# Q and K by DMA transpose, all inputs in 384-byte rows, and K^T V a unit ahead, in a gated linear attention + maxout kernel

## Chip, cores and metric

One core of one Trainium2 chip. The time is the device time of one execution in microseconds (us); lower is better. A run whose time is over 1.5% above the fastest of the same kernel is called slow, and ratios use the fast runs alone.

## The reference

Per batch and head, a 48 x 48 state is decayed by alpha and fed by the outer product of k and v at each of 768 steps; y is q times the state. The result, as 3072 tokens of 384 values, goes through a maxout layer.

```python
def _attn_ref(q, k, v, alpha):                     # (4, 8, 768, 48) each
    for t in range(S):
        state = alpha[:, :, t, :, None] * state + einsum('bhd,bhe->bhde', k[:, :, t], v[:, :, t])
        y[:, :, t] = einsum('bhd,bhde->bhe', q[:, :, t], state)
def _moe_ref(x, w1, w2, w_out):                    # (3072, 384), d_ff 1024
    return np.maximum(x @ w1, x @ w2) @ w_out
```

## The kernel before

The work is cut into 12 units of 256 tokens (two chunks of 128). A unit's chain: Ln of alpha on ScalarE; cumulative sums by matmul with masks; Exps; K and Q scaled (GpSimd, VectorE); **transposes of K and Q on TensorE**; pairs K Q^T ("pp", TensorE), masked on VectorE; K^T V for the state; y ("ya"); y transposed ("xp"); and, for the unit before, the hidden layer ("hp", 4 groups, each emptied by a Relu) and the output ("op"). The program order on each engine is fixed by hand, and all loads are issued by SyncE, four units ahead.

From unit 2 on, K and Q are loaded in 192-byte rows, so that each lands with one chunk on 128 partitions; alpha, V and the first units come in 384-byte rows (two tokens a row).

```python
def load_rows(u, name, src, cc):                   # 192-B rows: K, Q of units >= 2
    ...
    for j in range(2):
        nc.sync.dma_start(out=t[name][64 * j : 64 * j + 64, cc],
            in_=rows(src, u, cc * C, C).rearrange("h (p j) d -> j p h d", j=2)[j])

def turn(u, cc):                                   # 8 TensorE transposes and a PSUM copy
    tp = new(f"g{cc if u else 2 + cc}", [128, 2, HP, C], FP16, 1, "tp")
    for n, src in ((1, X["kn"][cc]), (0, X["qn"][cc])):
        for j in range(HP):
            nc.tensor.transpose(tp[:, n, j, :], pair(src, j), ident)
    ...

for u in range(2, NU):                             # one turn
    if u + 4 < NU:
        load(u + 4)
    kvmm(u, 0); pmm(u, 0); ...                     # K^T V, pairs of unit u
    hid(u - 1, 0); hid(u - 1, 1)                   # hidden layer of unit u-1
    sumd(u + 1); hid(u - 1, 2); sumc(u + 1); ...   # sums and Exps of unit u+1
    pmm(u, 1); ystate(u); ...
    hid(u - 1, 3, True)
    ...                                            # K, Q of u+1 scaled
    outp(u - 1, 0); yin(u)
    turn(u + 1, 0); turn(u + 1, 1)                 # transposes of unit u+1
    ...
```

## Time and profile before

| | before |
|---|---|
| time, median (range) | 146.35 us (145.24 to 147.23), 3 runs |
| span of the profiled run | 143.6 us |
| mean granted TensorE clock | 1.00 |
| TensorE busy | 94% |
| DMA queue of SyncE, share of 16 engines | 85.9% |

I call a **turn** the time from the first matmul of one unit's sums ("cs<-halves") to that of the next. In before, the turns of the loop (u = 2 to 9) take 9.66, 9.66, 9.77, 9.76, 9.76, 9.60, 9.59, 9.59 us.

### The profile page before, as it was taken

Reading aid. Unit: us, or ns where it says so; the run is one execution under the profiler, and the core shown is the slowest. Engines: PE = TensorE matmul, PEld = TensorE weight load, DVE = VectorE, ACT = ScalarE, POOL = GpSimd, SP = SyncE. Lnnn points to the kernel's source line nnn. Section 1 sums busy time; section 2 is a strip of 40 time slices with the busy share of each in tenths; the row PEclk is TensorE's granted clock in tenths of the full one; section 3 lists DMA queues with packets and bytes.
Section 4 is the critical chain, followed back from the end, with each engine's and each line's share of the span. In section 5 each row is a group of like instructions: output and inputs, shape, how many; then the busy total and the mean of one; then the engine's idle time right before and its main releaser. Section 6 shows DMA issues by size and latency. Waiting matters only on the chain.

```text
span 143.6 us, 4259 instructions
## 1 busy us (share of the span) xinstructions
PE 134.4 (94%) x1689; PEld 97.1 (68%) x1689; DVE 87.4 (61%) x180; ACT 97.1 (68%) x200; POOL 56.6 (39%) x111
## 2 busy tenths in 40 slices
PE   6868879998999999999999999999999999999991
PEld 2335544764877767877877777778777777776770
DVE  6048892865976757766767677556675755571110
ACT  3467642398788688687786975896879767655520
POOL 7491442066436154182291461631913616310000
PEclk9999999999999999999999999999999999999999
DMA  3999999978999999997998989999999785020203
GB/s 98 271 360 321 296 370 347 264 126 184 226 152 254 167 277 178 194 187 136 253 206 172 290 141 206 269 172 294 155 214 242 134 246 226 0 110 5 110 0 110
DMA packets 76483, 28.58 MB, mean 199 GB/s; under 512 B 71728, under 2 KB 74672, under 8 KB 76464
## 3 DMA queue, kind: packets, MB, share of 16 engines
q1 hardware_dynamic: 76320, 28.22, 85.9%
q8 instruction: 13, 0.21, 0.6%
q10 hardware_dynamic: 144, 0.10, 0.2%
q14 instruction: 6, 0.05, 0.1%
HBM read 23.59 MB, written 4.72 MB: 197 GB/s over the span
## 4 chain that ended last, share of the span: by engine, by line
PE 76%; SPq 10%; DMA 6%; ACT 3%; DVE 1%; issue 1%; ACTq 0%
PE hp L410 23%; PE op L435 20%; PE op L429 8%; SPq L75 6%; PE tp L296 6%; DMA w1f<-in_moe_w_dram 6%; PE pp L345 4%; PE ya L381 3%; PE cs L237 3%; PE xp L397 3%; PE kv L318 2%; SPq L115 2%; SPq L121 1%; PE ya L369 1%; PE cs L223 1%; ACT gT L415 1%
## 5 line engine op out<-in xcount | busy, mean ns | idle before, releaser
L415 ACT ACTIVATE gT<-hp 128x512 f16<-128x512 f32 x47 | 28.1, 597 | 16.2 <-PE hp L410 15.5
L410 PE MATMUL hp<-xt,w 128*128 128x256 f16 x288 | 37.4, 273 | 0.4 <-DVE w L498 0.2
L351 DVE TENSOR_TENSOR pt<-pp,um 128x512 f16<-128x512 f32 x48 | 30.9, 686 | 9.7 <-PE pp L345 9.4
L435 PE MATMUL op<-wo,gT 128*128 128x384 f16 x184 | 34.0, 326 | 0.0
L285 POOL TENSOR_TENSOR kn<-kf,Em 128x384 f16<-128x384 f32 x24 | 23.4, 996 | 24.8 <-ACT Em L247 24.8
L410 PEld LDWEIGHTS <-w 128*128 128x128 f16 x288 | 25.9, 97 | 5.3 <-issue 0.9
L435 PEld LDWEIGHTS <-gT 128*128 128x128 f16 x184 | 17.5, 98 | 10.5
L277 POOL TENSOR_TENSOR sb<-tm,dd 128x192 f16<-128x192 f32 x20 | 10.1, 506 | 32.5 <-DVE tm L331 20.2
L439 ACT COPY outs<-op 128x384 f32<-128x384 f32 x23 | 11.0, 477 | 13.7 <-PE op L435 13.7
L289 DVE TENSOR_TENSOR qn<-qf,cs 128x384 f16<-128x384 f32 x24 | 12.3, 550 | 13.0 <-ACT de L257 12.1
L331 DVE TENSOR_TENSOR tm<-kv,sb 64x192 f32<-64x192 f32 x32 | 11.3, 353 | 8.8 <-PE kv L318 7.9
L303 DVE COPY qk<-tp 128x1024 f16<-128x1024 f16 x20 | 12.9, 686 | 4.3 <-PE tp L296 4.3
L429 PE MATMUL op<-w2o,xt 128*128 128x384 f16 x69 | 15.0, 326 | 0.0
L205 POOL CAST v<-vf 64x384 f16<-64x384 f32 x24 | 12.0, 501 | 7.5 <-DMA vf<-in_v_dram 6.6
L207 ACT CAST v<-vf 64x384 f16<-64x384 f32 x24 | 12.2, 510 | 1.9 <-DMA vf<-in_v_dram 1.4
L247 ACT ACTIVATE Em<-cs 128x384 f32<-128x384 f32 x24 | 11.6, 485 | 2.5 <-PE cs L237 2.5
L193 ACT ACTIVATE lg<-af 128x768 f16<-128x768 f32 x12 | 10.1, 843 | 3.3 <-DMA af<-in_alpha_dram 3.0
L252 ACT ACTIVATE cs<-cs 128x384 f32<-128x384 f32 x24 | 11.8, 494 | 0.0
L504 PE MATMUL warm<-wz 128*128 128x512 f16 x30 | 10.0, 447 | 1.3 <-DVE halves L149 1.3
L388 ACT CAST xn<-ya 128x384 f16<-128x384 f32 x24 | 10.4, 492 | 0.0
L296 PE MATMUL tp<-ident,kn 128*128 128x128 f16 x96 | 9.3, 218 | 1.0 <-DVE qn L289 0.5
L345 PE MATMUL pp<-qk 48*128 48x128 f16 x192 | 9.8, 217 | 0.4 <-DVE qk L301 0.4
(66 smaller groups left out, 155.3 us busy)
## 6 DMA issues: line engine op xcount, KB each, us to landing
af<-in_alpha_dram SPq DMA_DIRECT2D x12, 384.0 KB, 5.6
vf<-in_v_dram SPq DMA_DIRECT2D x12, 384.0 KB, 5.0
out_dram<-outs SPq DMA_DIRECT2D x11, 384.0 KB, 5.1
kf<-in_k_dram SPq DMA_DIRECT2D x40, 96.0 KB, 4.7
qf<-in_q_dram SPq DMA_DIRECT2D x40, 96.0 KB, 4.3
w2f<-in_moe_w_dram SPq DMA_DIRECT2D x3, 512.0 KB, 6.0
wof<-in_moe_w_out_dram SPq DMA_DIRECT2D x2, 768.0 KB, 8.3
w1f<-in_moe_w_dram SPq DMA_DIRECT2D x4, 384.0 KB, 9.7
```

Source lines behind the costliest of these rows:

```text
L205: nc.gpsimd.tensor_copy(out=o, in_=i)
L207: nc.scalar.copy(out=o, in_=i)
L285: nc.gpsimd.tensor_mul(out=X["kn"][cc][:, :, 0:D], in0=part(u, "kf", cc), in1=X["Em"][cc])
L289: nc.vector.tensor_mul(out=X["qn"][cc][:, :, 0:D], in0=part(u, "qf", cc), in1=X["csv"][cc])
L296: nc.tensor.transpose(tp[:, n, j, :], pair(src, j), ident)
L303: nc.vector.tensor_copy(out=X["qk"][:, cc], in_=tp.rearrange("p n h t -> p (n h) t"))
L345: nc.tensor.matmul(pa[a][:, j, :], lhsT=qk[r, 1, j, :], rhs=qk[r, 0, j, :], start=True, stop=True)
L351: nc.vector.tensor_mul(out=pt[:, a], in0=X["pa", cc][a], in1=um.unsqueeze(1).to_broadcast([128, HP, C]))
L410: nc.tensor.matmul(hp[:, n, :], lhsT=w12[:, ds, f * 128 : (f + 1) * 128], rhs=X["xt"][:, ds].rearrange("p n t -> p (n t)"), start=(ds == 0 ...
L415: nc.scalar.activation(out=gT[:, 2 * f2 : 2 * f2 + 2, :], in_=hp, func=ACTF.Relu)
L429: nc.tensor.matmul(op, lhsT=X["xt"][:, ds, n, :], rhs=w2o[:, ds, :], start=(ds == 0), stop=False)
L435: nc.tensor.matmul(op, lhsT=X["gT"][:, f, n * C : (n + 1) * C], rhs=wo16[:, f, :], start=False, stop=(f == NF - 1))
```

## The change

Intent: take 16 transposes a unit (0.90 us) from TensorE, which bounds the kernel, by letting the DMA transpose K and Q from unit 3 on; load K and Q in the 384-byte rows that move faster; and compute K^T V a unit ahead, so that the state is there when y wants it. For the DMA transposes to land in time, sums and Exps of the next unit move to the head of a turn. Core of the diff (the loop cut to its order):

```diff
-    PAIRED = (0, 1)
+    BY_PE = (0, 1, 2)
...
-    def load_kq(u, cc):
-        load_rows(u, "kf", k, cc)
-        load_rows(u, "qf", q, cc)
+    def load_kq(u):
+        load_fat(u, "kf", k)
+        load_fat(u, "qf", q)
...
+                m = mf[:, j, i].rearrange("p c t -> p (c t)")
+                nc.tensor.matmul(csv[i], lhsT=m, rhs=lg[:, j, :, 0:D], start=(j == 0), stop=(j == 1))
...
+        if u in BY_PE:
+            ...
         else:
-            nc.vector.tensor_copy(out=X["qk"][:, cc], in_=tp.rearrange("p n h t -> p (n h) t"))
+            for cc in range(2):
+                nc.sync.dma_start(
+                    out=X["qk"][:, cc, :, 64 * i : 64 * i + 64],
+                    in_=X["kq"][64 * cc : 64 * cc + 64, i].rearrange("p n h w -> p (n h w)"), transpose=True,
+                )
...
     for u in range(2, NU):
         if u + 4 < NU:
-            load(u + 4)
+            load_a(u + 4)
+            load_kq(u + 4)
         if nxt:
-            sumd(u + 1)
+            sums(u + 1)
             expm(u + 1, 0)
             expp(u + 1, 0)
             expm(u + 1, 1)
+        pmm(u, 0)
...
+        hid(u - 1, 0, True)
+            kmul(u + 1, 0); qmul(u + 1, 0); expp(u + 1, 1); turn(u + 1, 0)
+        hid(u - 1, 1, True)
+            kmul(u + 1, 1); qmul(u + 1, 1); turn(u + 1, 1); expd(u + 1)
...
+        hid(u - 1, 2, True)
+        pmm(u, 1)
+            kvmm(u + 1)
+        if u + 4 < NU:
+            load_v(u + 4)
         hid(u - 1, 3, True)
...
-                ln(u + 2)
+        if u + 3 < NU:
+            ln(u + 3)
```

(Before the loop, `ln(3)` and `ln(4)`. The lines with semicolons stand for several of the diff. The rows of two tokens also ask for a third copy of V in every unit, on GpSimd, in unit 3 on VectorE.)

More of the change, by code (lines that the diff above doesn't have):

```diff
@@ L78, in load_fat @@
         )
-    def load_rows(u, name, src, cc):
-        t = st[u]
-        if name not in t:
-            t[name] = ldp.tile([128, 2, H, D], FP32, tag=name, name=name)
-        for j in range(2):
-            nc.sync.dma_start(
-                out=t[name][64 * j : 64 * j + 64, cc],
-                in_=rows(src, u, cc * C, C).rearrange("h (p j) d -> j p h d", j=2)[j],
-            )
     def load_a(u):
@@ L94, in load_v @@
         load_fat(u, "vf", v)
-    def load_kq(u, cc):
-        load_rows(u, "kf", k, cc)
-        load_rows(u, "qf", q, cc)
+    def load_kq(u):
+        load_fat(u, "kf", k)
+        load_fat(u, "qf", q)
     def load(u):
         load_a(u)
-        if u in PAIRED:
-            load_fat(u, "kf", k)
-            load_fat(u, "qf", q)
-        else:
-            load_kq(u, 0)
-            load_kq(u, 1)
+        load_kq(u)
         load_v(u)
@@ L116 @@
     load_a(1)
-    load_fat(1, "kf", k)
-    load_fat(1, "qf", q)
+    load_kq(1)
     for n in range(2):
@@ L154 @@
     NB = 3
-    LG, QN, KN = [], [], []
+    LG, KQ = [], []
     for n in range(NB):
@@ L170 @@
         )
-    for n in range(2 * NB):
-        for lst, nm in ((QN, "qn"), (KN, "kn")):
-            t = constp.tile([128, H, P64], FP16, name=f"{nm}{n}")
-            nc.vector.memset(t[:, :, D:P64], 0.0)
-            lst.append(t)
+    for n in range(NB):
+        t = constp.tile([128, 2, 2, H, P64], FP16, name=f"kq{n}")
+        nc.vector.memset(t.rearrange("p i n h w -> p (i n h) w")[:, :, D:P64], 0.0)
+        KQ.append(t)
     w2h = wp.tile([128, ND, DFF], FP16)
@@ L207, in vcast @@
                 nc.scalar.copy(out=o, in_=i)
-                if u in PAIRED:
-                    nc.gpsimd.tensor_copy(out=X["v16"][64 * cc : 64 * cc + 64, 2], in_=i)
+                (nc.vector if u == 3 else nc.gpsimd).tensor_copy(out=X["v16"][64 * cc : 64 * cc + 64, 2], in_=i)
     def sums(u):
@@ L231, in sumc @@
             for i in range(2):
-                if u in PAIRED:
-                    m, x = mf[:, j, i].rearrange("p c t -> p (c t)"), lg[:, j, :, 0:D]
-                else:
-                    r = slice(64 * i, 64 * i + 64)
-                    m, x = mc[r, j], lg[r, j, :, 0:D]
-                nc.tensor.matmul(csv[i], lhsT=m, rhs=x, start=(j == 0), stop=(j == 1))
-        X["qn"], X["kn"], X["Em"] = [], [], []
-        for cc in range(2):
-            X["qn"].append(QN[(2 * u + cc) % (2 * NB)])
-            X["kn"].append(KN[(2 * u + cc) % (2 * NB)])
+                m = mf[:, j, i].rearrange("p c t -> p (c t)")
+                nc.tensor.matmul(csv[i], lhsT=m, rhs=lg[:, j, :, 0:D], start=(j == 0), stop=(j == 1))
+        X["kq"], X["Em"] = KQ[u % NB], []
+        X["qn"], X["kn"] = ([X["kq"][:, i, n] for i in range(2)] for n in range(2))
     def expm(u, cc):
@@ L277, in state, with kmul, qmul @@
         nc.gpsimd.tensor_mul(out=X["sb", cc], in0=tm, in1=dd.unsqueeze(2).to_broadcast([128, HP, D]))
-    def part(u, name, i):
-        return st[u][name][:, :, i, :] if u in PAIRED else st[u][name][:, i]
-    def kmul(u, cc):
+    def kmul(u, i):
         X = st[u]
-        nc.gpsimd.tensor_mul(out=X["kn"][cc][:, :, 0:D], in0=part(u, "kf", cc), in1=X["Em"][cc])
-    def qmul(u, cc):
+        nc.gpsimd.tensor_mul(out=X["kn"][i][:, :, 0:D], in0=X["kf"][:, :, i, :], in1=X["Em"][i])
+    def qmul(u, i):
@@ L288, in qmul, with turn @@
         X = st[u]
-        nc.vector.tensor_mul(out=X["qn"][cc][:, :, 0:D], in0=part(u, "qf", cc), in1=X["csv"][cc])
-    def turn(u, cc):
+        nc.vector.tensor_mul(out=X["qn"][i][:, :, 0:D], in0=X["qf"][:, :, i, :], in1=X["csv"][i])
+    def turn(u, i):
         X = st[u]
-        tp = new(f"g{cc if u else 2 + cc}", [128, 2, HP, C], FP16, 1, "tp")
-        for n, src in ((1, X["kn"][cc]), (0, X["qn"][cc])):
-            for j in range(HP):
-                nc.tensor.transpose(tp[:, n, j, :], pair(src, j), ident)
-        if cc == 0:
-            X["qk"] = gp.tile([128, 2, 2 * HP, C], FP16, tag="qk", bufs=2, name="qk")
-        if u in PAIRED:
-            o = X["qk"].rearrange("p c n (j t) -> p j n c t", j=2)[:, cc]
+        if i == 0:
+            X["qk"] = gp.tile([128, 2, 2 * HP, C], FP16, tag="qk", bufs=2, name="qk")
+        if u in BY_PE:
+            tp = new(f"g{i if u else 2 + i}", [128, 2, HP, C], FP16, 1, "tp")
+            for n, src in ((1, X["kn"][i]), (0, X["qn"][i])):
+                for j in range(HP):
+                    nc.tensor.transpose(tp[:, n, j, :], pair(src, j), ident)
+            o = X["qk"].rearrange("p c n (j t) -> p j n c t", j=2)[:, i]
@@ L301, in turn, with kvmm @@
             nc.vector.tensor_copy(out=o, in_=tp.rearrange("p n h (c t) -> p (n h) c t", c=2))
         else:
-            nc.vector.tensor_copy(out=X["qk"][:, cc], in_=tp.rearrange("p n h t -> p (n h) t"))
-    def kvmm(u, cc):
+            for cc in range(2):
[3 more added lines that the diff above has]
+                )
+    def kvmm(u):
@@ L306, in kvmm @@
         X = st[u]
-        X["kvp", cc] = kvp = new(f"g{3 - cc}", [128, HP, 2 * D], FP32, 1, "kv")
+        for cc in range(2):
+            X["kvp", cc] = new(f"g{3 - cc if u in BY_PE else 1 - cc}", [128, HP, 2 * D], FP32, 1, "kv")
         for j in range(HP):
-            if u in PAIRED:
-                r = slice(64 * cc, 64 * cc + 64)
-                for i in range(2):
+            for i in range(2):
+                for cc in range(2 if more(u) else 1):
+                    r = slice(64 * cc, 64 * cc + 64)
@@ L312, in kvmm @@
                     nc.tensor.matmul(
-                        kvp[:, j, :], lhsT=pair(X["kn"][i][r], j),
+                        X["kvp", cc][:, j, :], lhsT=pair(X["kn"][i][r], j),
                         rhs=X["v16"][r, cc if i == cc else 2, 2 * j : 2 * j + 2, :],
@@ L316, in kvmm @@
                     )
-            else:
-                nc.tensor.matmul(
-                    kvp[:, j, :], lhsT=pair(X["kn"][cc], j), rhs=X["v16"][:, cc, 2 * j : 2 * j + 2, :],
-                    start=True, stop=True,
-                )
     def kvsum(u, cc):
@@ L333, in kvsum, with kvsums @@
                 nc.vector.tensor_copy(out=tm[r], in_=kvp[r, :, e])
+    def kvsums(u):
+        kvsum(u, 0)
+        state(u, 1)
+        if more(u):
+            kvsum(u, 1)
     def more(u):
@@ L528 @@
     wturn(0)
-    kvmm(0, 0)
-    kvmm(0, 1)
+    kvmm(0)
     kvsum(0, 0)
@@ L581 @@
     outp(0, 0)
-    kvmm(1, 0)
-    kvmm(1, 1)
+    kvmm(1)
     kvsum(1, 0)
@@ L599 @@
     xturn(1)
+    ln(3)
     vcast(2)
     outg(0, 1, (4, 5, 6, 7))
-    ln(3)
     load(5)
+    ln(4)
     for u in range(2, NU):
@@ L608 @@
         if u + 4 < NU:
-            load(u + 4)
-        kvmm(u, 0)
-        pmm(u, 0)
-        kvsum(u, 0)
-        pmask(u, 0)
-        state(u, 1)
-        if more(u):
-            kvmm(u, 1)
-        hid(u - 1, 0)
-        hid(u - 1, 1)
+            load_a(u + 4)
+            load_kq(u + 4)
         if nxt:
-            sumd(u + 1)
-        hid(u - 1, 2)
-        if nxt:
-            sumc(u + 1)
+            sums(u + 1)
             expm(u + 1, 0)
@@ L626 @@
             expm(u + 1, 1)
-        if more(u):
+        pmm(u, 0)
+        if u in BY_PE:
+            kvmm(u)
+        else:
+            ystate(u)
+        pmask(u, 0)
+        if u in BY_PE:
+            kvsum(u, 0)
+            state(u, 1)
+        hid(u - 1, 0, True)
+        if nxt:
+            kmul(u + 1, 0)
+            qmul(u + 1, 0)
+            expp(u + 1, 1)
+            turn(u + 1, 0)
+        hid(u - 1, 1, True)
+        if nxt:
+            kmul(u + 1, 1)
+            qmul(u + 1, 1)
+            turn(u + 1, 1)
+            expd(u + 1)
+            state(u + 1, 0)
+        if u in BY_PE:
             kvsum(u, 1)
+            vcast(3)
+        hid(u - 1, 2, True)
         pmm(u, 1)
-        ystate(u)
+        if nxt:
+            kvmm(u + 1)
         pmask(u, 1)
+        if nxt:
+            kvsums(u + 1)
+        if u + 4 < NU:
+            load_v(u + 4)
         hid(u - 1, 3, True)
-        if nxt:
-            expp(u + 1, 1)
-            expd(u + 1)
-            for cc in range(2):
-                kmul(u + 1, cc)
-                qmul(u + 1, cc)
-            state(u + 1, 0)
         outp(u - 1, 0)
+        if u in BY_PE:
+            ystate(u)
         yin(u)
-        if nxt:
-            turn(u + 1, 0)
-            turn(u + 1, 1)
         outx(u - 1, 1)
-        if nxt:
-            xturn(u)
-            vcast(u + 1)
-            if u + 2 < NU:
-                ln(u + 2)
-            outg(u - 1, 1)
-        else:
-            outg(u - 1, 1, (0, 1, 2, 3))
-            xturn(u)
-            outg(u - 1, 1, (4, 5, 6, 7))
+        outg(u - 1, 1, (0, 1, 2, 3))
+        xturn(u)
+        if u + 2 < NU:
+            vcast(u + 2)
+        outg(u - 1, 1, (4, 5, 6, 7))
+        if u + 3 < NU:
+            ln(u + 3)
     for f2 in range(4):
```

## The prediction

> **What bounds the kernel now.** I read the page first, then the chain of work in time order, then busy time by window, then the SyncE queue in time order. The page:
>
> ```profile
> PE 134.4 (94%) x1689; PEld 97.1 (68%) x1689; DVE 87.4 (61%) x180; ACT 97.1 (68%) x200; POOL 56.6 (39%) x111
> ...
> DMA  3999999978999999997998989999999785020203
> ...
> q1 hardware_dynamic: 76320, 28.22, 85.9%
> ```
>
> Two things are full, not one: TensorE (94%), and the DMA engines, which are at 9 tenths from slice 2 to slice 34 and idle after. The chain that ended last is TensorE in every steady unit. One of them, in time (start, us, what):
>
> ```profile
> 58.24 1.31 PE hp L410 x12
> 59.73 0.68 PE hp L410 x6
> 60.40 0.43 PE cs L237 x4
> ...
> 63.81 0.40 PE ya L381 x16
> 64.21 0.90 PE tp L296 x16
> 65.11 0.49 PE op L429 x3
> ...
> 68.01 1.31 PE hp L410 x12
> ```
>
> Each unit of 256 tokens starts 9.76 us after the one before (58.24 to 68.01; from unit 8 on 9.59), with no gap in TensorE. The 16 transposes of Q and K are 0.90 us of it: that is what the change takes away. The DMA side, by window (length, busy us of PE, PEld, DVE, ACT, POOL, clock, DMA share, GB/s):
>
> ```profile
> 12.00:16.00 4.00, 3.86 (x58) 2.56 (x57) 3.80 (x8) 2.56 (x3) 0.51 (x1) 1.00 1.24 271
> 26.00:28.00 2.00, 2.00 (x17) 1.46 (x15) 1.61 (x3) 1.13 (x2) 0.00 (x0) 1.00 1.26 263
> 28.00:34.00 6.00, 5.78 (x63) 3.44 (x62) 3.78 (x8) 4.82 (x10) 2.71 (x6) 1.00 0.81 141
> 62.00:66.00 4.00, 4.00 (x55) 3.07 (x53) 2.71 (x6) 3.27 (x9) 3.27 (x7) 1.00 0.79 142
> ```
>
> While 384-B rows move alone (12 to 16, 26 to 28 us) the rate is about 265 GB/s; while the 192-B rows of K and Q move alone (28 to 34, 62 to 66 us) it is 141. Both are about 700 rows per us, so a row costs the same at either size. The pace of the loads, read from the issues of alpha on the SyncE queue:
>
> ```profile
> 69.14 0.43 SPq L75 DMA_DIRECT2D af<-in_alpha_dram  x1
> 78.74 0.43 SPq L75 DMA_DIRECT2D af<-in_alpha_dram  x1
> 87.56 0.42 SPq L75 DMA_DIRECT2D af<-in_alpha_dram  x1
> 96.79 0.43 SPq L75 DMA_DIRECT2D af<-in_alpha_dram  x1
> 106.77 0.43 SPq L75 DMA_DIRECT2D af<-in_alpha_dram  x1
> ```
>
> The last is unit 11's. In program order it belongs to the turn of the loop that starts at 87.5 us, so it goes out 19 us late, and its pace (9.4 us a unit) is only just TensorE's. Prefetch four units deep hides this today: nothing in the steady part waits long for a load.
>
> **What the Trainium skill says.** (1) "DMA: Bandwidth & Descriptors", Queues, rings and completion order: on each DMA engine the descriptors of one issuing queue are taken in ring order. So a transpose issued by SyncE moves only after the loads issued ahead of it. The trace of before has no transpose, but its constant lag of the loads is such a backlog. (2) The same page, Latency and other measured facts: a DMA transpose reached 261 GB/s on one kernel. No run here shows it yet. (3) "TensorEngine Tiling (Array Packing)", Key Properties: matmuls on different row tiles run in parallel. The trace agrees: four 64-row matmuls of 384 columns take 0.33 us (TensorE starts at 60.34 and goes on at 60.67), where three 128-row ones of 384 columns take 0.49.
>
> **The change part by part.** *Transposes off TensorE*, units 3 to 11: 9 x 0.90 = 8.1 us gone; DVE loses two PSUM copies of 0.69 us per unit, off the path. *Cumulative sums* with 128-row masks: no longer in parallel pairs, 4 x 0.163 = 0.65 in place of 0.33, for 10 units: +3.2. *K^T V*: 16 matmuls of 64 rows, in parallel pairs over the two chunks, so still 0.33 us for units 2 to 7; in the last four units one chunk alone is wanted and 8 unpaired ones take 0.33 in place of 0.17: +0.6. Sum on TensorE: -8.1 + 3.2 + 0.6 = -4.3 us, which alone would give 142.1.
>
> *The new order on ACT.* Sums of the next unit now come first in a turn, and the Exps sit ahead of the Relus. ScalarE's order is: copy of the output, Ln, Exp, Exp, Exp, Relu. The spacings of before:
>
> ```profile
> 60.94 0.49 ACT L247 ACTIVATE Em<-cs 128x384 f32<-128x384 f32 x1
> 61.32 0.49 ACT L252 ACTIVATE cs<-cs 128x384 f32<-128x384 f32 x1
> 61.73 0.48 ACT L247 ACTIVATE Em<-cs 128x384 f32<-128x384 f32 x1
> 62.10 0.59 ACT L415 ACTIVATE gT<-hp 128x512 f16<-128x512 f32 x1
> ```
>
> From the end of the last output matmul: 0.20 until the copy starts, 0.41 copy, 0.81 Ln, 0.38 + 0.41 + 0.37 for three Exps, 0.60 Relu: 3.17 us. TensorE reaches the third pair of hidden matmuls, which needs the PSUM buffer that this Relu empties, after 0.85 (sums) + 0.30 + 0.30 + 2 x 0.66 = 2.77. So it waits some 0.45 us a turn, plus about 0.05 before K^T V for the last Exp and the product with Q: 0.5 x 8 turns = +4.0. The gain shrinks to about nothing.
>
> *DMA.* K and Q of ten units in 384-B rows: a load of 393 KB takes 1.5 us at 265 GB/s in place of 2.8 at 141. A unit costs 4 x 1.5 + about 1 for its output = 7.0 in place of 9.6, plus four transposes of 131 KB each: at 261 GB/s 0.5 us each, 2 us. So 9.0 a unit: no relief to speak of. And these transposes have no slack: unit u+1's must land before its pairs (one turn later), and they stand in SyncE's order behind alpha, K and Q of unit u+4. For the first, unit 3's, I count the queue from 28.2 us, where K and Q of unit 2 begin (the fall from 263 to 141 GB/s): three loads of unit 2, four each of units 3, 4 and 5, three of unit 6 = 18 loads x 1.48 = 26.7 us, and one output, 1 us: 56 us. Then 2 us for the transposes and 1.5 us, as for the small outputs at the end, to land: 59 us. TensorE wants them at 48.9 us (1 us into the turn that began at 47.9), or at about 51, since Ln of unit 4 now stands ahead of unit 3's Exps and its alpha lands near 41. If the rows go 10% faster, or SyncE's lead of 3 us lets the transposes slip ahead, it is 53 to 56. So one wait of 5 to 10 us at the third unit, and from there DMA (9.0 plus the landing time) and TensorE (9.2 to 9.6) go about level, as SyncE also holds the loads behind the output of the turn before.
>
> Sum: 146.35 - 4.3 + 4.0 + (5 to 10) = 151 to 156. I take 152.
>
> **The rivals.** *TensorE's saving stays whole*: 142 to 143. For it: the chain is TensorE all through, and leaving units 0 to 2 on TensorE looks like a choice made with a profile in hand. Against it: the late loads in the SyncE queue, and ScalarE's 3.17 us. *The saving goes to ScalarE's order, and the transposes come in time*: 145 to 147. For it: the count on ScalarE needs nothing unknown; against: the transposes would have to pass the loads. *The transposes wait behind the loads* (my choice): 149 to 156. *They are also slow*, 1 us or more each, and pace the five units that still load: 5 x 2 us more, 158 or over. The page "VectorE: DVE Perf Modes", The three transpose paths, gives 1309 ns for a 128x128 block by DMA; that is mostly one transfer's latency, I think, so I give this little weight.
>
> **Range and chances.** The second and third rival span 145 to 156; the first adds a tail below, the last a tail above: 144 to 159. Faster by over 2% is below 143.4, which needs the first rival nearly whole: 0.20. Within 2%: 0.19. Slower: 0.61.
>
> **What would show each step.** Right: a wait of TensorE (the pairs' weight load) on the DMA of the transposed tile at unit 3, near 50 us and several us long; DMA rate about 265 GB/s from 28 us on; third hidden pair waiting for a Relu some 0.4 us in each turn; units 9 to 11 at about 9.5 us. Wrong: no wait of the pairs on a DMA, transposes landing within 3 us of issue, turns of 9.1 us. If the transposes are served beside the loads and not behind them, or if 384-B rows go well over 300 GB/s when nothing else is queued, my main term falls.

## The result, and the profile after

| | before | after |
|---|---|---|
| time, median (range), 4 runs each | 146.55 us (145.24 to 147.23) | 171.55 us (170.87 to 175.45; that one slow) |
| span of the profiled run | 143.6 us | 169.3 us |
| mean granted TensorE clock | 1.00 | 0.929 |

The result is correct. The median of the three fast runs of after is 171.18. The ratio of fast runs is 1.170 (95%: 1.159 to 1.182): **slower by 17%**, above the range predicted (144 to 159). A ratio is the mean time of one kernel's fast runs over that of the other's in the same rounds, so not quite the ratio of the medians.

The page of after, with the lines that answer those of before, and the row of the granted clock (in before it is 9 in all 40 slices; a slice of after is 4.2 us):

```profile
PE 140.9 (83%) x1609; PEld 94.8 (56%) x1609; DVE 76.3 (45%) x155; ACT 96.7 (57%) x200; POOL 65.5 (39%) x129
...
PEclk9999999999659759975999999968999999999999
DMA  5999999999999978979979989989997254442022
...
q1 hardware_dynamic: 74464, 32.94, 87.4%
```

TensorE has 80 instructions fewer and yet is busy longer, for some of it runs at half clock; it is idle 28 us of the span where it was idle 9. The DMA engines are at 7 tenths or more until 131 us, in before until 118. Queue 1 moved 32.94 MB in place of 28.22: the 4.72 MB more are the 36 transposes of 131 KB.

The waits of after, by total time (us in total, times, longest):

```profile
PE pp L323 <- DMA qk<-kq: 12.4, 5, 5.0
...
ACT lg L176 <- DMA af<-in_alpha_dram: 6.2, 3, 3.3
...
PE hp L388 <- ACT gT L393: 4.0, 3, 3.4
```

So the pairs waited for the transposed tile five times, as much as 5 us. The turns say when (us):

| turn u | 2 | 3 | 4 | 5 | 6 | 7 | 8 | 9 |
|---|---|---|---|---|---|---|---|---|
| before | 9.66 | 9.66 | 9.77 | 9.76 | 9.76 | 9.60 | 9.59 | 9.59 |
| after | 16.15 | 16.19 | 15.56 | 9.64 | 11.52 | 13.78 | 10.77 | 9.64 |

The differences sum to 25.9 us; the spans differ by 25.7. What lies outside cancels: turn 2 starts 2.0 us earlier in after (38.05 against 40.06), as the sums now stand first in a turn, and from turn 10 to the end it takes 28.0 against 26.1. So the loss lies in these turns. The last turn, and turn 5, show the new order when nothing is late: 9.64 us, no shorter than before.

In the lines below L323 (L345 in before) is the pairs, L388 the hidden layer, L276 the DMA transposes, L74 the loads and L421 the output. TensorE in time, the first pairs of unit 3 in before and then three groups of after (start, us, what, in brackets the idle time before and what ended it):

```profile
47.91 0.40 PE L345 MATMUL pp<-qk 48*128 48x128 f16 x8
```

```profile
44.56 1.44 PE L388 MATMUL hp<-xt,w 128*128 128x256 f16 x6 [3.41 <-ACT gT L393]
...
60.26 0.61 PE L323 MATMUL pp<-qk 48*128 48x128 f16 x8 [5.05 <-DMA qk<-kq]
...
61.52 3.29 PE L388 MATMUL hp<-xt,w 128*128 128x256 f16 x18
```

Unit 3's pairs start 12.35 us later than before (60.26 against 47.91). From them to the end of the span it is 109.0 us after and 95.7 before: 13.35 more. These two sums are the 25.7 us, and they have one cause, which the SyncE queue shows. Its order in time (start, us, what) in after:

```profile
53.67 5.99 SPq L276 DMA_TRANSPOSE qk<-kq  x4
...
78.94 6.31 SPq L276 DMA_TRANSPOSE qk<-kq  x4
85.30 0.58 SPq L74 DMA_DIRECT2D vf<-in_v_dram  x1
86.65 0.36 SPq L421 DMA_DIRECT2D out_dram<-outs  x1
87.06 1.50 SPq L74 DMA_DIRECT2D af<-in_alpha_dram  x1
88.60 0.70 SPq L74 DMA_DIRECT2D kf<-in_k_dram  x1
89.35 1.88 SPq L74 DMA_DIRECT2D qf<-in_q_dram  x1
91.40 5.94 SPq L276 DMA_TRANSPOSE qk<-kq  x4
...
102.59 7.03 SPq L276 DMA_TRANSPOSE qk<-kq  x4
...
115.06 6.82 SPq L276 DMA_TRANSPOSE qk<-kq  x4
```

From one group to the next there is hardly a gap. The queue issues without rest (from 53.67, where unit 3's transposes go out, to 123.1 no gap reaches 0.8 us), and **four transposes of a unit take 5.7 to 7.0 us of it**; the median of one is 1.27 us. Only the first of the four takes longer while loads stand ahead of it (1.8 to 3.1 us); the other three take 1.20 to 1.29 each. Four loads and an output of other units take the rest. The first transposes of units 3 and 8 start at 53.67 and 115.06, so the queue's pitch is (115.06 - 53.67) / 5 = **12.28 us a unit**, against 9.6 to 9.8 of TensorE. From the start of its issue to its landing a transpose takes 3.0 us in the median. Five pitches are 5 x (12.28 - 9.64) = 13.2 us over TensorE's pace: the 13.35.

The second wait of the table of waits is one of turn 2. ScalarE in after:

```profile
42.02 0.84 ACT L176 ACTIVATE lg<-af 128x768 f16<-128x768 f32 x1 [3.29 <-DMA af<-in_alpha_dram]
```

Ln of unit 4 stands ahead of unit 3's Exps and Relus, and its alpha lands at 42.0. So the Relu is late, and TensorE's third hidden group waits 3.41 us (44.56 above). During such a wait, and during that of 5.05 us, the granted clock falls. By window (length; busy us of PE, PEld, DVE, ACT, POOL; clock, DMA share, GB/s):

```profile
43.40:50.20 6.80, 5.34 (x41) 3.25 (x41) 5.05 (x12) 4.18 (x10) 4.22 (x8) 0.50 1.13 281
...
137.00:140.00 3.00, 3.00 (x35) 1.96 (x33) 0.99 (x3) 1.62 (x4) 1.76 (x4) 1.00 0.60 91
```

Four stretches (43.4 to 50.3, 57.1 to 63.9, 74.2 to 81.0 and 111.7 to 115.1) are at half clock, 23.9 us together. The second line is the end of the kernel, where transposes move alone: 91 GB/s, at 0.60 of the DMA engines' time.

### The profile page after: what moved, and what is told of

It reads as the page before. It is cut to its first block, busy times and chain, and to the rows that moved or that the text cites. A ratio compares the mean times of both kernels' runs of the same rounds, so it can differ in the third digit from the quotient of the medians.

```text
span 169.3 us, 4078 instructions
## 1 busy us (share of the span) xinstructions
PE 140.9 (83%) x1609; PEld 94.8 (56%) x1609; DVE 76.3 (45%) x155; ACT 96.7 (57%) x200; POOL 65.5 (39%) x129
## 3 DMA queue, kind: packets, MB, share of 16 engines
q1 hardware_dynamic: 74464, 32.94, 87.4%
HBM read 23.59 MB, written 4.72 MB: 167 GB/s over the span
## 4 chain that ended last, share of the span: by engine, by line
PE 47%; DMA 18%; SPq 13%; ACT 7%; issue 6%; POOL 4%; DVE 3%; ACTq 0%; POOLq 0%; DVEq 0%
PE hp L388 19%; PE op L413 11%; DMA qk<-kq 9%; SPq L74 5%; DMA w1f<-in_moe_w_dram 5%; PE op L407 5%; SPq L276 5%; DMA af<-in_alpha_dram 4%; PE pp L323 3%; ACT gT L393 2%; PE ya L359 2%; PE kv L289 2%; POOL v L191 2%; ACT Em L223 2%; PE ya L347 1%
## 5 line engine op out<-in xcount | busy, mean ns | idle before, releaser
L388 PE MATMUL hp<-xt,w 128*128 128x256 f16 x288 | 43.0, 302 | 4.5 <-ACT gT L393 4.0
L388 PEld LDWEIGHTS <-w 128*128 128x128 f16 x288 | 29.0, 107 | 13.8 <-issue 6.1
L413 PE MATMUL op<-wo,gT 128*128 128x384 f16 x184 | 35.6, 327 | 0.0
L257 POOL TENSOR_TENSOR kq<-kf,Em 128x384 f16<-128x384 f32 x24 | 23.4, 995 | 28.1 <-issue 17.7
L323 PE MATMUL pp<-qk 48*128 48x128 f16 x192 | 10.7, 232 | 12.9 <-DMA qk<-kq 12.4
L261 DVE TENSOR_TENSOR kq<-qf,cs 128x384 f16<-128x384 f32 x24 | 13.0, 550 | 16.1 <-ACT cs L228 10.3
L253 POOL TENSOR_TENSOR sb<-tm,dd 128x192 f16<-128x192 f32 x20 | 10.1, 506 | 23.1 <-DVE tm L303 12.0
L377 DVE COPY xt<-xp 128x768 f16<-128x768 f16 x12 | 6.7, 556 | 24.1 <-PE xp L375 24.1
L323 PEld LDWEIGHTS <-qk 48*128 48x128 f16 x192 | 6.1, 99 | 20.2 <-issue 15.4
L188 POOL CAST v<-vf 64x384 f16<-64x384 f32 x24 | 12.0, 501 | 5.8 <-DMA vf<-in_v_dram 5.2
L176 ACT ACTIVATE lg<-af 128x768 f16<-128x768 f32 x12 | 10.1, 844 | 6.4 <-DMA af<-in_alpha_dram 6.2
L190 ACT CAST v<-vf 64x384 f16<-64x384 f32 x24 | 12.2, 510 | 1.2 <-DMA vf<-in_v_dram 0.8
L251 POOL TENSOR_TENSOR dd<-de 128x4 f32<-128x4 f32 x20 | 4.1, 203 | 20.2 <-ACT de L233 19.9
L191 POOL CAST v<-vf 64x384 f16<-64x384 f32 x22 | 11.1, 503 | 1.0
```

The costliest lines, as they stand in the source:

```text
L188: nc.gpsimd.tensor_copy(out=o, in_=i)
L190: nc.scalar.copy(out=o, in_=i)
L191: (nc.vector if u == 3 else nc.gpsimd).tensor_copy(out=X["v16"][64 * cc : 64 * cc + 64, 2], in_=i)
L257: nc.gpsimd.tensor_mul(out=X["kn"][i][:, :, 0:D], in0=X["kf"][:, :, i, :], in1=X["Em"][i])
L261: nc.vector.tensor_mul(out=X["qn"][i][:, :, 0:D], in0=X["qf"][:, :, i, :], in1=X["csv"][i])
L323: nc.tensor.matmul(pa[a][:, j, :], lhsT=qk[r, 1, j, :], rhs=qk[r, 0, j, :], start=True, stop=True)
```

## The experiments

Three theories, with the letters that the expectations use:

- **A**: the DMA transposes are late, because of the SyncE queue. Narrowed later, with a digit: by their place behind the loads (A1); by the work of a turn as a whole, in whatever order (A2); or by sharing one issuing queue with the loads (A3).
- **B**: the half clock after waits is itself a large part of the loss.
- **C**: the new order on ScalarE and TensorE (Ln far ahead, sums first) costs it, whoever transposes.

"Pitch" below is the mean spacing of the first transposes of units 3 to 8 on the SyncE queue (12.28 in after). Three batches of four kernels, each batch on one chip; before in the same rounds: 146.02 (e1 to e4), 145.88 (e5 to e8), 146.09 (e9 to e12), 7 runs each.

| run | time, us | ratio to before (95%) | turns 2 to 9, us | pitch |
|---|---|---|---|---|
| after | 171.55 | 1.170 (1.159 to 1.182) | 16.15 16.19 15.56 9.64 11.52 13.78 10.77 9.64 | 12.28 |
| e1, transposes on TensorE | 160.55 | 1.099 (1.093 to 1.105) | 16.99 10.83 10.83 10.83 10.83 10.53 10.53 10.53 | - |
| e2, Ln later | 176.19 | 1.206 (1.198 to 1.213) | 15.73 19.15 11.46 14.87 11.00 10.99 12.84 10.99 | 12.21 |
| e3, no late loads (wrong data) | 153.03 | 1.047 (1.039 to 1.055) | 16.36 10.35 9.64 9.64 9.64 9.64 9.64 9.64 | 9.58 (from unit 5 on 9.64, TensorE's) |
| e4, clock held up | 171.34 | 1.171 (1.164 to 1.178) | 14.58 17.25 12.84 12.45 12.24 12.28 11.69 9.64 | 12.18 |
| e5, transposes ahead of the loads | 165.52 (its one fast run) | - | profiled slow | 12.15 (slow run) |
| e6, loads issued by GpSimd | 166.22 | 1.140 (1.132 to 1.148) | 18.48 15.58 10.23 10.47 10.80 12.89 9.64 9.64 | 11.19 |
| e7, two transposes for four | 164.64 | 1.129 (1.122 to 1.135) | 17.03 16.38 9.65 11.58 12.65 9.64 10.32 9.64 | 11.21 |
| e8, half the bytes (wrong data) | 166.03 (its one fast run) | - | 17.27 15.61 9.64 12.13 10.70 13.37 10.19 9.64 | 11.70 |
| e9, before with the rows alone | 149.90 | 1.026 (1.022 to 1.031) | 10.21 10.21 10.32 10.31 10.31 10.09 10.09 10.09 | - |
| e10, e1 with turn 2 mended | 155.86 | 1.067 (1.063 to 1.071) | 12.65 10.84 10.84 10.84 10.84 10.53 10.53 10.53 | - |
| e11, after with turn 2 mended | 171.45 | 1.174 (1.168 to 1.179) | 11.65 20.94 15.43 9.64 11.07 13.67 10.85 9.64 | 12.22 |
| e12, e3 and Ln ahead of a copy (wrong data) | 151.00 | 1.033 (1.028 to 1.039) | 16.81 9.98 9.38 9.38 9.38 9.38 9.38 9.38 | - |

### e1: the transposes back on TensorE, the rest of the change kept

```diff
-        if u in BY_PE:
+        if True:
...
+        if nxt:                       # after yin(u), as in before
+            turn(u + 1, 0)
+            turn(u + 1, 1)
```

> The changed kernel with Q and K of every unit turned by TensorE (at the place where the kernel before had it); everything else of the change stays. Theory A (the DMA transposes are the loss: each takes about 1.27 us of the SyncE queue, behind the loads, and TensorE waits for their landing): no wait of the pairs on a DMA, granted clock near 1.0 from unit 3 on; what stays is the 3.4 us wait of the turn of unit 2 for the Ln of unit 4 with its slow clock, and turns of 10.0 to 10.5 us: 150 to 158 us. Theory C (the new order of work and the sums in 128-row masks are the loss, whatever turns Q and K): 165 us or more.

160.55 us: 10.6 below the fast runs of after and 14.5 above before, just outside A's numbers and well short of C's. So both have a part: the DMA transposes cost some 11 us net, although each turn with transposes on TensorE is 10.83 us (10.53 from turn 7 on), 1.19 (0.89) more than the 9.64 of turns whose DMA transposes are in time. Of the 14.5, turn 2 has 7.3, and the other turns 1.07 (turns 3 to 6) and 0.94 (7 to 9).

### e2: Ln a unit later

```diff
-    ln(4)                             # ahead of the loop
...
-        if u + 3 < NU:
-            ln(u + 3)
+        if u + 2 < NU:
+            ln(u + 2)
```

> The changed kernel with each Ln one unit later in the order (unit 4's no longer ahead of the Exps of unit 3). Theory A: the turn of unit 2 loses its 3.4 us wait, but the transposes of unit 3 stand at the same place in the queue and land at the same 60 us, so the wait at unit 3 grows from 5 to about 10 us and the total stays within 2 us of 171.5. Theory C (the order on ScalarE costs time of its own): 5 to 6 us faster, about 166.

A miss of both forecasts: 176.19 us, slower still. The pitch is 12.21, as in after, so the queue is no faster. Ln now stands just ahead of the sums that read it, and TensorE waits for it each turn:

```profile
53.99 0.35 PE L205 MATMUL cs<-halves,lg 128*128 128x4 f16 x8 [1.44 <-ACT lg L176]
```

Turn 2 remains 15.7 us, since K^T V of unit 3 then waits 2.20 us for GpSimd's cast of V and the clock halves. That shows why Ln was put so far ahead, and that turn 2 had a second cause. e10 and e11 mend both.

### e3: no loads in the loop (wrong)

Units 6 on take the tiles of four units before in place of a load; the result is wrong, the work of the engines the same.

```diff
         if u + 4 < NU:
-            load_a(u + 4)
-            load_kq(u + 4)
+            st[u + 4] = {n: st[u][n] for n in ("af", "kf", "qf", "vf")}
...
-        if u + 4 < NU:
-            load_v(u + 4)
```

> The changed kernel without the loads of units 6 to 11 (they compute on the tiles of units 2 to 5 again, so the result is wrong on purpose); all DMA transposes stay. Theory A, as shared queue: the transposes of unit 3 land near 56 us in place of 61, later ones land in time, turns of 9.6 to 10 us: 152 to 158 us. If the transposes are too slow even alone (rival: their own latency, not what stands ahead of them), turns stay at 11 us or more and the total above 163.

153.03 us, as A expected. From turn 4 on every turn is 9.64, and turn 3 is 10.35: without the loads behind and ahead of them the transposes are in time. But they're not cheap. The SyncE queue and TensorE in the same turn of e3:

```profile
77.61 5.15 SPq L276 DMA_TRANSPOSE qk<-kq  x4
```

```profile
77.59 0.81 PE L388 MATMUL hp<-xt,w 128*128 128x256 f16 x6 [0.29 <-ACT gT L393]
```

Even alone a unit's four transposes hold the queue 5.15 us, 1.29 each. They are issued by 82.8, the last lands at about 84.3, and TensorE starts the pairs at 84.9: little to spare. The second line is the third hidden group's wait for a Relu: 0.29 us a turn.

### e4: the clock held up with dummy matmuls

```diff
+    def pads(u, cc, n):               # n matmuls of zeros into the pairs' buffer, ahead of the pairs
+        ...
+        for _ in range(n):
+            nc.tensor.matmul(pa[0].rearrange("p h t -> p (h t)"), lhsT=wz[:, 0:128], rhs=wz, start=True, stop=True)
...
+        pads(u, 0, {3: 30, 4: 16, 5: 8, 6: 8, 7: 8, 8: 8}.get(u, 0))
         pmm(u, 0)
...
+        pads(u, 1, 14 if u == 2 else 0)
         hid(u - 1, 2, True)
```

> The changed kernel with matmuls on zeros put ahead of the waits of TensorE in the turns of units 2 to 8, which write PSUM that the pairs overwrite. The waits themselves stay. Theory B (after each wait of several us TensorE runs at half the granted clock for 3 to 7 us, 24 us in all, and this is a third of the loss): mean clock from 0.93 to 0.98 or more, total down by 5 to 9 us, 163 to 166. If only the landing times count and the half clock is hidden in them: 170 to 173.

The clock was 1.00 in the profiled run, and the time the same: 171.34 us. By window:

```profile
57.10:63.90 6.80, 5.52 (x47) 3.20 (x46) 1.90 (x4) 1.16 (x3) 0.00 (x0) 1.00 0.86 151
```

B falls: the same time at full clock. A faster TensorE reaches the next late transpose sooner and waits longer. Turns 4 to 7 are now 12.2 to 12.8 us each, plainly the queue's pitch (12.18).

### e5: the transposes ahead of the loads

```diff
-        if u + 4 < NU:
-            load_a(u + 4)
-            load_kq(u + 4)
...
         if u + 4 < NU:
-            load_v(u + 4)
+            load(u + 4)
```

> The changed kernel with the loads of alpha, K and Q of unit u+4 issued after the transposes of the turn and not before them; same work, other place in the SyncE queue. Theory A1 (place: what stands ahead of the transposes makes them late): unit 3's land near 56 us in place of 61, later ones within their turn; the total falls to 155 to 163. Theory A2 (throughput: transposes, loads and output together are 12.2 us of queue a turn, in whatever order): the turns of units 3 to 8 stay near 12 us, only the first wait shrinks: 166 to 171.

Three of its four runs fell in the slow state (median of all 168.32), the profiled one too, so no ratio is given and the trace is read with care; its one fast run took 165.52, some 6 us below after and just under A2's range. In the profiled run unit 3's transposes go out at 49.18 in place of 53.67, and turn 3 is 10.16 us; but turns 4 to 7 are 11.0 to 13.6 us and the pitch is 12.15, as in after. So far as this one slow profile shows, place in the queue moves the first transposes by 4.5 us and not the pitch.

### e6: the loads of units 5 on issued by GpSimd

```diff
-        nc.sync.dma_start(
+        (nc.gpsimd if u >= 5 else nc.sync).dma_start(
```

> The changed kernel with the loads of units 5 to 11 issued by GpSimd, so on another queue than the transposes. If it is SyncE's issue of the transposes (1.27 us each, 5.1 us a turn) in series with the loads that paces the turns (A3), they now go side by side: turns near 10 us, total 150 to 160. If the DMA engines themselves are full (A2), turns stay near 12 us: 165 to 173. GpSimd's own cost of issuing may add to either.

166.22 us, between the two forecasts. The pitch falls to 11.19, so sharing one queue is a part of it. What is left is no longer the SyncE queue's throughput:

```profile
75.77 5.14 SPq L276 DMA_TRANSPOSE qk<-kq  x4
82.84 0.33 SPq L421 DMA_DIRECT2D out_dram<-outs  x1
85.89 5.85 SPq L276 DMA_TRANSPOSE qk<-kq  x4
```

A unit's transposes still take 5.14 to 7.69 us of it, but over the five pitches it is held 31.7 of 55.9 us and stands idle for the rest, mostly waiting for the product with Q on VectorE or for an output. GpSimd pays for the issues: 0.88 to 0.92 us for each load, and its cast of V waits 7.38 us for V in turn 2, which is 18.5 us long.

### e7: two transposes of 64 x 2048 in place of four of 64 x 1024

K and Q of both parities lie side by side, so that one transpose takes a chunk.

```diff
-        t = constp.tile([128, 2, 2, H, P64], FP16, name=f"kq{n}")
+        t = constp.tile([128, 2, HP, 2, 2, P64], FP16, name=f"kq{n}")
...
-        else:
+        elif i == 1:
             for cc in range(2):
                 nc.sync.dma_start(
-                    out=X["qk"][:, cc, :, 64 * i : 64 * i + 64],
-                    in_=X["kq"][64 * cc : 64 * cc + 64, i].rearrange("p n h w -> p (n h w)"), transpose=True,
+                    out=X["qk"][:, cc].rearrange("p n (i t) -> p (n i) t", i=2),
+                    in_=X["kq"][64 * cc : 64 * cc + 64].rearrange("p n j i a w -> p (n j i a w)"), transpose=True,
```

> The changed kernel with two DMA transposes of 64 x 2048 a unit in place of four of 64 x 1024 (K and Q of both parities beside each other in the source); same bytes. If a transpose costs by its bytes: 2.5 us each on the SyncE queue, 5 us a unit as before, and the total stays at 170 to 174 (a bit later, as the first half can't start early). If it costs by the instruction: 1.3 us each, 2.6 us a unit, turns of about 9.8 us, total 157 to 162.

164.64 us, correct, the fastest correct variant that transposes by DMA, though between the two forecasts (157 to 162, 170 to 174). The queue, first while loads flow and then alone:

```profile
65.42 4.36 SPq L278 DMA_TRANSPOSE qk<-kq  x2
...
129.69 3.25 SPq L278 DMA_TRANSPOSE qk<-kq  x2
```

Alone, the same bytes hold the queue 3.25 us in two instructions (1.25 and 1.95) and 5.15 in four (e3): the number of instructions counts. The bytes show in the landing: with no load about it comes 2.5 us after the end of an issue, 1.5 in e3 and 1.1 in e8 (half the bytes). The pitch falls by 1.07.

### e8: half the bytes in four instructions (wrong)

Half of the heads are transposed; the pairs read them twice.

```diff
-                    out=X["qk"][:, cc, :, 64 * i : 64 * i + 64],
-                    in_=X["kq"][64 * cc : 64 * cc + 64, i].rearrange("p n h w -> p (n h w)"), transpose=True,
+                    out=X["qk"][:, cc, 0:HP, 64 * i : 64 * i + 64],
+                    in_=X["kq"][64 * cc : 64 * cc + 64, i, 0].rearrange("p n h w -> p (n h w)"), transpose=True,
```

> The changed kernel with four DMA transposes of 64 x 512 a unit: only half of the heads are turned, the other half reads their tiles again, so the result is wrong on purpose; TensorE's work is the same. If a transpose costs by its bytes: 0.65 us each, 2.6 us a unit, 9.7 us of queue a turn, total 157 to 163 (what is left over before is the turn of unit 2 and the first wait). If by the instruction: no change, 169 to 173.

```profile
64.77 5.68 SPq L278 DMA_TRANSPOSE qk<-kq  x4
...
130.11 5.05 SPq L278 DMA_TRANSPOSE qk<-kq  x4
```

A transpose of 64 x 512 holds the queue as long as one of 64 x 1024: 5.05 us for four, alone, against 5.15. Up to 131 KB it is a **price by the instruction**, about 1.26 us. The transfer of the bytes doesn't fill that time: from 130.2 to 135.1 us the DMA engines' share is 0.23. The pitch does fall by 0.58, of which the transposes' time on the queue gives 0.27 a unit and the loads' 0.24. One of its two runs was slow, so no ratio; the fast one took 166.03, again between the two forecasts.

### e9: the kernel before with the 384-byte rows alone

```diff
-    PAIRED = (0, 1)
+    PAIRED = tuple(range(12))
```

> The kernel before with K and Q of all units in 384-B rows by chunk and pair (parity beside), so with the 128-row masks for the sums, 64-row matmuls for K^T V and the third copy of V on GpSimd, but with its own order and TensorE turning Q and K. My count on TensorE: sums +0.32 us a unit for ten units; K^T V in its old order is not paired over the chunks, +0.33 (units 2 to 7) or +0.17 (8 to 11): 5.9 us in all, 151 to 153, with no wait on a DMA. If the DMA backlog of before cost time that I did not see: 149 or less. If the layout costs more on GpSimd or VectorE: 155 or more.

149.90 us, 3.8 over before; a miss, my count of 5.9 was too high. Each turn is 0.50 to 0.55 us longer (by the count: full-height sums, and K^T V in twice as many matmuls that find no partner in before's order), with no wait for a DMA. The rows do what they were meant to. The DMA row of e9's page (a slice is 3.7 us):

```profile
DMA  4999999999999999999995985952002020020202
```

The last load lands at 100 us in place of 118. But before did not wait for loads, so this is off the path and buys nothing.

### e10: e1 with turn 2 mended

Ln of unit 4 and the state product of unit 2 go behind unit 3's Exps and K product in turn 2.

```diff
-    ln(4)
...
-            state(u, 1)
...
             expd(u + 1)
+            if u == 2:
+                state(2, 1)
+                ln(4)
```

> The kernel of the first experiment (all of the change, TensorE turns Q and K) with the turn of unit 2 repaired: the Ln of unit 4 after the Exps of unit 3 in that turn and no longer ahead of the loop, and the state product of unit 2 after the products of K of unit 3 on GpSimd. If the 7 us that the turn of unit 2 loses come from these two waits (alpha of unit 4 still loading; GpSimd late with V of unit 3): turn of 10.5 to 12 us in place of 17.0, total 154 to 156. If loads not yet landed (V of unit 3) hold it anyway: 158 or more.

155.86 us as expected, though turn 2 falls from 16.99 to 12.65 only (10.5 to 12 expected); the clock is 1.00. With TensorE setting the pace, mending turn 2 is worth 4.7 us. So the rows and the new order lose 9.8 us with no DMA transpose at all; e9 puts 3.8 of it down to the rows, and the rest was not taken apart.

### e11: the same mend on after

The edit of e10, on the changed kernel.

> The same repair on the changed kernel itself (DMA transposes). Theory A (the transposes' place in the queue and the pace of 12 us a turn set the time): the pairs of unit 3 still start at 60 to 61 us, the wait grows by what the turn of unit 2 saves, total 170 to 173. If the losses add up: 164 to 167.

```profile
60.45 0.61 PE L323 MATMUL pp<-qk 48*128 48x128 f16 x8 [9.60 <-DMA qk<-kq]
```

171.45 us: nothing gained. Turn 2 is 4.5 us shorter, and the wait at unit 3 is 9.60 in place of 5.05; its pairs start at 60.45 (60.26 in after), for the queue reaches the first transposes at 53.84 (53.67). So C's part in after is hidden behind A's: turn 2 only decides which wait it is put down to.

### e12: e3, and Ln ahead of the last output copy (wrong)

```diff
-        outg(u - 1, 1, (4, 5, 6, 7))
         if u + 3 < NU:
             ln(u + 3)
+        outg(u - 1, 1, (4, 5, 6, 7))
```

(on top of e3's edit)

> The changed kernel without the loads of units 6 to 11 (wrong result on purpose, 9.64 us a turn) with Ln ahead of the copy of the last output on ScalarE and not behind it. My prediction put 0.45 us of TensorE's wait a turn down to this order: then 9.2 to 9.4 us a turn, the total 2 to 3 us below the 153.0 of that kernel. If the wait for the Relu is set by something else: 9.6 us a turn.

```profile
75.51 2.33 PE L388 MATMUL hp<-xt,w 128*128 128x256 f16 x18
```

The three hidden groups run without a wait, and the turn is 9.38 us as expected: the 0.29 us of e3 was ScalarE's order, Ln between the copy and the Exps.

**What follows from all twelve.** A holds, and by throughput (A2): what a unit asks of the SyncE queue (pitch 12.28) is more than TensorE's turn (9.64). From 53.67 to 115.06 us the queue of after is held 58.5 of 61.4 us; a unit's 12.28 are 6.2 for its transposes, 5.0 for four loads, 0.5 for an output and 0.6 between them. The 16 DMA engines moved 204 GB/s in that stretch, and 231 in that of e6; in e8 their share fell from 1.00 to 0.83 and the pitch by only 0.58 (with loads alone the share reads 1.24, so 1.00 is not its top). Three means lower the pitch by a part each: another queue (-1.1), half as many instructions (-1.1), half the bytes (-0.6); they were not tried together, and only taking the loads away makes the transposes harmless. No correct run with DMA transposes came near before. Two things remain open: what sets the pitch of 11.19 in e6, where the SyncE queue has idle time, and what the 1.26 us is spent on; the trace shows only that the queue is held.

No run is faster than before. e12's turn of 9.38 is 0.2 to 0.4 us below before's, and it is to be had only where no load flows (units 9 to 11): under 1 us in all, by this estimate.

## Why the prediction was wrong

Taken by its own steps:

- **Bounds of before**: right. Two things were full, and the DMA was the one to look at.
- **The 384-byte rows at about 265 GB/s**: right, 248 to 283 from 30 to 55 us in after.
- **TensorE's sum, -4.3 us, and ScalarE's order, +4.0**: the balance near zero was right, in turns where nothing is late; the two terms were not measured apart. A turn with its transposes in time is 9.64 us (predicted 9.2 to 9.6), against 9.59 to 9.77 before. ScalarE's gap at the third hidden group was 0.29 us, predicted 0.45 (the prediction's own 3.17 - 2.77 gives 0.40).
- **The first transposes land at 59 us**: near, by luck. They went out at 53.67 (counted 56) and took 6.0 and not 2 us; the two errors nearly cancel, and the pairs started at 60.26.
- **"So one wait of 5 to 10 us at the third unit"**: the wait was at the right place, and the delay 12.35 us. Part of it shows as turn 2's wait for Ln of unit 4 (3.41 us; the prediction put alpha's landing near 41, it was 42.0) and the half clock around it; e11 shows that this is the same delay under another name. The bare difference of the prediction's own times, 59 - 48.9, is 10.1, so the range was cut short at its upper end.
- **The step that failed**: "plus four transposes of 131 KB each: at 261 GB/s 0.5 us each, 2 us. So 9.0 a unit", and from it "from there DMA (9.0 plus the landing time) and TensorE (9.2 to 9.6) go about level". One transpose holds the queue 1.27 us and a unit's four 5.15 us alone and 5.7 to 7.0 (mean 6.2) beside loads. The unit's work is 12.28 us, not 9.0: the transposes 6.2 for 2, the loads and the output 5.5 for 7.0, and 0.6 of gaps for none (time on the queue, where the prediction counted transfer time). The mechanism (a queue in order, transposes behind loads) was right; the transposes' term was mis-sized by 4.2 us and the sum by 3.3, over five pitches. With TensorE at 9.64 that is 13.2 us that the sum lacked, and 12.35 + 13.35 is the 25.7 measured.
- **The rivals**: the fourth, "They are also slow, 1 us or more each ... 158 or over", is what happened (13.2 us over five units, where it said 10). I dismissed its evidence, 1309 ns for a block by DMA, as "mostly one transfer's latency". The measured 1.27 us is nearly that figure, it is paid by the instruction even for eight blocks of 64x128, and it holds the queue; alone (e3) the landing comes 1.5 us after the end of the issue, as the prediction said. A rate from another kernel was used, and the one number for a small transpose was put aside; that it comes so near for this other size may be chance.
- **Clock**: not foreseen. It showed in the trace (0.929) and cost nothing here (e4).

## What to carry to other kernels

Before moving work to a DMA queue, count what the queue spends by the instruction, not only bytes over a rate, and add it to all that the same queue issues in one period; then compare that with the period of the engine relieved. Here 0.90 us of TensorE was traded for over 5 us of a queue that was already near full (in before, loads and outputs held it 47.0 of 50.2 us from 57.0 to 107.2). And a wait that is mended ahead of a later, independent one can gain nothing (e11), just as a halved clock may cost nothing (e4): the pitch of the resource that is behind tells which.

## What the Trainium skill lacked or had wrong

- "DMA: Bandwidth & Descriptors", Latency and other measured facts, gives 261 GB/s for a DMA transpose. Here, in pieces of 131 KB, it was 102 GB/s (131 KB in 1.29 us of the queue, e3) and 91 GB/s in the window at the end of after. What the page lacks is a time measured on trn2 for which one such transpose, SBUF to SBUF, holds the issuing queue: here about 1.26 us for 66 and for 131 KB alike, with the landing 1.1 and 1.5 us after it when nothing else moves.
- "Advanced Engine Details and Errata", X-Bar Transpose (TRN2), says that these transposes "are as fast as regular DMAs". In these pieces they were not: loads alone moved at about 265 GB/s (before), transposes of 131 KB alone at 91.
- "TensorE: Matmul & The Clock Gate", Part 1, states that the clock is halved after an idle window of about 3.4 us. The trace agrees in part: each of the four stretches at 0.50 lasted 6.8 or 3.4 us. But the clock fell 2.3, 1.9 and 2.7 us into the waits of 3.41, 5.05 and 3.52 us, and the fourth time after waits of 2.10 and 0.58 us. So in these records less than 3.4 us of unbroken idle time was enough; how idle a window must be, the page doesn't say.
